# Block-diagonal scores for the last query tile, copies of keys on GpSimd, and 20 instead of 50 unread products

## The chip, the cores and the metric

The kernel runs on one core of one Trainium2 chip. The metric is the device time of one launch in microseconds. The engines are named as in the profile: PE (TensorE, products), PEld (its weight loads), DVE (VectorE), ACT (ScalarE), POOL (GpSimd) and SP (SyncE, which issues the DMAs).

## What is computed

Four batches of eight heads attend over 576 positions with a head size of 64 and a decay term, then two dense layers follow. Cut to what matters:

```
scores = scale * q @ k^T;  cum = cumsum(log(clip(f)))
scores = where(causal, -1e9, scores + cum[:, None] - cum[None, :])
attn = softmax(scores);  x = (attn @ v), heads side by side: 2304 x 512
h = x @ w_in;   g = h * clip(h + 3, 0, 6) / 6;   x = g @ w_out        # first layer, 512 -> 2048 -> 512
h = x @ w_in2;  g = piecewise square of h;       out = g @ w_out2     # second layer
```

## The kernel before, in words

**Attention.** The 576 queries of a head are cut at 256. The lower half of a batch gives four jobs of kind "two" (two heads, query tiles 0 and 1), the upper half gives for each pair of heads two jobs of kind "one" (one head, tiles 2 and 3) and one of kind "last". The fifth tile has 64 queries of each head only, so "last" handles both heads of a pair in one 128-row tile. There are 16 jobs of kind "two", 32 "one" and 16 "last". The 16 "two" jobs run their scores as fp32 products (`sc<-kn,qn`).

**Split operands.** In the upper halves an fp32 number is a rounded fp32r part (qh, the high part) and a rest (ql). A tile kk holds the 64 rows of the rounded keys above the 64 rows of their rest, and q stands twice above itself in qh and ql, so qh times kk gives qh·k_high + qh·k_rest in one product of 128 rows. A "last" tile needs qh and ql for two heads: q of each head was padded with zero columns to 128 columns (behind the 256 of qraw, hence the width QW), and four products for each half of the 288 keys add up to the scores: eight products 128x288 for a pair of heads.

**Dense layers.** `moe_h` makes a 128-wide piece of the hidden layer out of 12 products into a bank hp, ACT and DVE turn it into two parts g, and `moe_o` adds them into the output banks o. Weights come as raw 64-bit data and are split by ACT and DVE (`w_split`, wr and w).

**Order.** The program is written out as a list of pieces, and then `plan` records all instructions, builds their dependences (`graph`), gives each a cost in ns and lets a list scheduler (`schedule`) set the order on each engine, which the engines keep. `cost` and `late` are those of the planner. "held" names tiles whose DMA the planner may not put ahead of the PE instruction that stands before it in the program. SPARE products that nobody reads (`spare<-upper,lf`) are set by the planner where it sees PE idle. They share the two banks of `ps_h` with hp: as long as one is still to come, only one bank is free for hp. The dense products start once pairs 0 to 4 of the attention are through (av, then xt); the dense work of the first layer is interleaved with the rest of the attention.

Of the kernel before, what the change touches and what calls it, by code (L numbers as in the profile page):

```python
# [8 lines left out]
F32 = mybir.dt.float32  # L9
F32R = mybir.dt.float32r  # L10
# [6 lines left out]
P = 128  # L17
# [16 lines left out]
NATS = 16  # L34
QW = S - QA + (S - 4 * 128)
DB = 3
NORMS = 12
FIRST = 8
EARLY = 6
SPARE = 50  # L40
AHEAD0 = 1
# [59 lines left out]
def graph(nc, homes, follows, held=()):  # L101
# [119 lines left out]
    for k, i in enumerate(ops):  # L221
# [154 lines left out]
def tile_kernel(  # L376
# [83 lines left out]
    def w_split(kind, c, half, s, raw):  # L460
        if kind == "parts":
# [5 lines left out]

        nc.scalar.activation(out=rf, in_=hw.bitcast(F32), func=AF.Abs)  # L468
        nc.vector.tensor_scalar(
            out=rf, in0=rf, scalar1=2.0 ** -15, scalar2=122880.0,  # L470
            op0=ALU.max, op1=ALU.min,
        )
        nc.vector.tensor_scalar(
            out=t, in0=t, scalar1=5, scalar2=2, op0=ALU.logical_shift_left, op1=ALU.logical_shift_right
        )
        nc.vector.scalar_tensor_tensor(
            out=t, in0=hw, scalar=-1073741824, in1=t, op0=ALU.bitwise_and, op1=ALU.bitwise_or
        )
        nc.vector.scalar_tensor_tensor(  # L479
            out=t, in0=lw, scalar=29, in1=t,  # L480
            op0=ALU.logical_shift_right, op1=ALU.bitwise_or,
        )
        hi, lo = wsb[half][s][:, 0], wsb[half][s][:, 1]
# [26 lines left out]
    nc.gpsimd.memset(pt4, 0.0)  # L510

    def v_load(p):
        d = pairs[p]
# [7 lines left out]
    def u_load(n):  # L521
# [4 lines left out]
        if kind == "last":  # L526

            d["dec"] = att.tile([P, S], F32, tag="dec", name="dec", bufs=DB)
            for y in range(2):
                nc.sync.dma_start(out=d["dec"][y * D:(y + 1) * D], in_=ncum[r + y:r + y + 1, :].to_broadcast([D, S]))  # L530
            return
        q0, nq, nk = (0, QA, QA) if kind == "two" else (QA, S - QA, S)
# [9 lines left out]
        else:  # L542
            kraw = att.tile([P, S], F32, tag="kraw", name="kraw", bufs=1)
            qraw = att.tile([P, QW], F32, tag="qraw", name="qraw", bufs=1)
            for y in range(2):
# [3 lines left out]
                )  # L549
            if kind == "one":  # L550

                o = QA + W4 * (h % 2)
                nc.gpsimd.memset(qraw[:, S - o:S - o + W4], 0.0)
                nc.sync.dma_start(out=qraw[:, 0:QA], in_=q[b, h, :, q0:q0 + QA])
                nc.sync.dma_start(out=qraw[:, o:o + W4], in_=q[b, h, :, q0 + QA:S])
            d.update(kraw=kraw, qraw=qraw)
        w = nk if kind == "two" else 4 * P
        dec = att.tile([P, S], F32, tag="dec", name="dec", bufs=DB)
        if n < DECS:
            t = bank("dc")  # L560
            for y in range(nh):
                ty = t[:, y * QA:(y + 1) * QA]
                for c in range(QA // P):
# [3 lines left out]
                    )  # L567
            rounded("v", dec[:, 0:nh * nk], t[:, 0:nh * nk])
        else:
# [5 lines left out]
    def u_split(n):  # L575
# [3 lines left out]
        if kind == "last":  # L579
# [8 lines left out]
            )  # L588
            rounded("p", end[D:P], dm[D:P, 0:W4])
        else:  # L590

# [7 lines left out]
            if not d["nat"]:  # L599
# [4 lines left out]
                ql = att.tile([P, QW], F32R, tag="ql", name="ql", bufs=3)  # L604
                w, x = nh * d["nk"], 2 * QA if kind == "two" else QA + P
                rounded("a", kk[:, 0:w], kraw[:, 0:w])
                rest("v", kk[D:P, 0:w], kraw[D:P, 0:w], kk[D:P, 0:w])
                rounded("a", qh[:, 0:x], qraw[:, 0:x])
                rest("v", ql[:, 0:x], qraw[:, 0:x], qh[:, 0:x])
                d.update(kk=kk, qh=qh, ql=ql)  # L610
# [18 lines left out]
    def u_scores(n, i):  # L629
# [5 lines left out]
        if kind == "last":  # L635
# [3 lines left out]
            ts = [bank("sc") for _ in halves]  # L639
            for part in ("qh", "ql"):  # L640
                for t, (a, e) in zip(ts, halves):
                    for y in range(2):
                        o = jobs[n - 2 + y]
                        nc.tensor.matmul(  # L644
                            t[:, 0:e - a], lhsT=o[part][:, QA:QA + P], rhs=o["kk"][:, a:e],
                            start=part == "qh" and y == 0, stop=part == "ql" and y == 1,
                        )
            softmax(d, 0, pr, [(t[:, 0:e - a], dec[:, a:e], a, e) for t, (a, e) in zip(ts, halves)])
# [33 lines left out]
    def u_norm(n):  # L682
# [17 lines left out]
    def u_trans(n, x):  # L700
# [12 lines left out]
        if kind == "two":  # L713
# [3 lines left out]
            for y in range(2):  # L717
                for z, i in enumerate(tl):
                    tr(y * w + z * P, prob[i], y * (i * P + P) + x * P)
            rounded("a", pt[:, x, :, x * P:QA], t[:, 0:2 * w].rearrange("p (h n) -> p h n", h=2))  # L720
# [282 lines left out]
    nc.sync.dma_start(out=lf0, in_=f0)  # L1003
    lf = att.tile([P, L], F32, tag="prob1", name="lf")


# [68 lines left out]
    for g in range(len(steps) + LAG):  # L1075
# [21 lines left out]
        else:  # L1097
# [46 lines left out]
```

## Time and profile before

| | |
|---|---|
| median of 3 runs | 1003.04 us (1000.57 to 1003.18) |
| the profiled execution | 1000.51 us, span of its instructions 998.8 us |
| PE busy | 989.3 us (99% of the span) |
| DVE busy | 577.3 us (58%) |
| ACT busy | 523.0 us (52%) |
| POOL busy | 75.6 us (8%) |
| DMA | 129 MB, 40.2% of the DMA engines' span in the main queue |

Busy times are those of the engine's instructions, without the sequencer's waits and issues. The busy time of PE is modelled at its ends, so hidden waits of some tenths of a microsecond can lie in it. An fp32 product leaves two records in the trace, an fp32r product one.

### The profile page before, as it was taken

Reading aid. Unit: us, or ns where it says so; the run is one execution under the profiler, and the core shown is the slowest. Engines: PE = TensorE matmul, PEld = TensorE weight load, DVE = VectorE, ACT = ScalarE, POOL = GpSimd, SP = SyncE. Lnnn points to the kernel's source line nnn. Section 1 sums busy time; section 2 is a strip of 40 time slices with the busy share of each in tenths; the row PEclk is TensorE's granted clock in tenths of the full one; section 3 lists DMA queues with packets and bytes.
Section 4 is the critical chain, followed back from the end, with each engine's and each line's share of the span. In section 5 each row is a group of like instructions: output and inputs, shape, how many; then the busy total and the mean of one; then the engine's idle time right before and its main releaser. Section 6 shows DMA issues by size and latency. Waiting matters only on the chain.

```text
span 998.8 us, 14754 instructions
## 1 busy us (share of the span) xinstructions
PE 989.3 (99%) x5110; PEld 799.2 (80%) x5110; DVE 577.3 (58%) x1375; ACT 523.0 (52%) x1192; POOL 75.6 (8%) x208
## 2 busy tenths in 40 slices
PE   8999999999999999999999999999999999999998
PEld 6766777777778777779988888888888888888897
DVE  7799677899763655555436489997222322322232
ACT  6988566667763656555523256674333333433343
POOL 2121100111110101100000002001000000000000
PEclk9999999999999999999999999999999999999999
DMA  6773669745565875238382337342000100100010
GB/s 195 218 205 115 178 208 295 249 138 151 175 218 208 247 221 155 84 104 271 111 325 78 103 106 240 130 164 77 11 1 27 43 1 1 42 6 1 1 43 22
DMA packets 67099, 129.05 MB, mean 129 GB/s; under 512 B 11728, under 2 KB 32464, under 8 KB 67024
## 3 DMA queue, kind: packets, MB, share of 16 engines
q1 hardware_dynamic: 67024, 128.11, 40.2%
q8 instruction: 40, 0.66, 0.3%
q14 instruction: 35, 0.29, 0.1%
HBM read 102.84 MB, written 25.24 MB: 128 GB/s over the span
## 4 chain that ended last, share of the span: by engine, by line
PE 96%; DVE 1%; DMA 1%; issue 1%; ACT 0%; POOL 0%; SPq 0%; DVEq 0%; ACTq 0%; POOLq 0%
PE hp L849 40%; PE o L899 20%; PE o L892 19%; PE pt L711 4%; PE av L753 4%; PE sc L669 3%; PE sc L659 2%; PE sc L644 2%; PE spare L1017 1%; PE dc L564 1%; DMA wraw<-in_w 0%; DVE prob L619 0%; DMA dec<-ncum 0%; DMA lf<-in_f 0%; DVE kk L431 0%
## 5 line engine op out<-in xcount | busy, mean ns | idle before, releaser
L849 PE MATMUL hp<-xt,w 128*128 128x512 f32 (+1 forms) x960 | 229.2, 377 | 0.7 <-DVE u L857 0.7
L892 PE MATMUL o<-g,w 128*128 128x512 f32 (+1 forms) x960 | 227.9, 376 | 0.1
L849 PE MATMUL hp<-x,w 128*128 128x512 f32 (+1 forms) x960 | 210.6, 368 | 0.0
L899 PE MATMUL o<-w,g 128*128 128x512 f32 x864 | 209.6, 389 | 0.0
L849 PEld LDWEIGHTS hp<-x,w 128*128 128x128 f32 x960 | 169.3, 188 | 31.2
L849 PEld LDWEIGHTS hp<-xt,w 128*128 128x128 f32 x960 | 163.7, 189 | 30.5 <-issue 2.8
L892 PEld LDWEIGHTS o<-g,w 128*128 128x128 f32 x960 | 164.5, 189 | 29.1 <-issue 1.7
L899 PEld LDWEIGHTS o<-w,g 128*128 128x128 f32 x864 | 161.1, 188 | 32.8
L861 DVE SCALAR_TENSOR_TENSOR u<-hp,u 128x512 f32<-128x512 f32 (+1 forms) x80 | 50.9, 637 | 166.6 <-ACT u L860 166.6
L431 DVE TENSOR_TENSOR g<-u,g 128x512 fp32r<-128x512 f32 (+1 forms) x160 | 102.2, 639 | 62.9 <-ACT g L423 36.7
L423 ACT ACTIVATE g<-u 128x512 fp32r<-128x512 f32 (+1 forms) x160 | 94.2, 589 | 77.3 <-DVE u L861 49.5
L859 ACT ACTIVATE u<-hp 128x512 f32<-128x512 f32 (+1 forms) x80 | 44.3, 554 | 155.8 <-PE hp L849 155.8
L625 ACT ACTIVATE prob<-prob,mx 128x128 f32<-128x128 f32 (+4 forms) x144 | 83.6, 582 | 53.2 <-DVE mx L619 52.5
L857 DVE SCALAR_TENSOR_TENSOR u<-u,hp 128x512 f32<-128x512 f32 (+1 forms) x80 | 50.5, 631 | 85.3 <-ACT u L856 85.0
L856 ACT ACTIVATE u<-hp 128x512 f32<-128x512 f32 (+1 forms) x80 | 44.1, 551 | 95.2 <-PE hp L849 94.8
L619 DVE CUSTOM_DVE_ANT_0 prob<-sc,dec 128x256 f32<-128x256 f32 (+2 forms) x112 | 55.2, 502 | 37.1 <-PE sc L669 28.9
L423 ACT ACTIVATE pt<-pt 128x512 f32<-128x512 f32 (+3 forms) x160 | 63.2, 433 | 24.4 <-PE pt L711 23.9
L711 PE MATMUL pt<-ident,prob 128*128 128x128 f32 (+1 forms) x400 | 64.3, 275 | 0.2
L711 PEld LDWEIGHTS pt<-ident,prob 128*128 128x128 f32 (+1 forms) x400 | 46.8, 139 | 16.5 <-issue 3.2
L423 ACT ACTIVATE w<-wr 128x512 fp32r<-128x512 f32 x64 | 40.3, 630 | 26.2 <-DVE wr L479 25.9
L753 PE MATMUL av<-pt,vv 128*64 128x320 f32 (+3 forms) x448 | 50.3, 364 | 0.0
L468 ACT ACTIVATE wr<-wraw 128x512 f32<-128x512 f32 x64 | 42.6, 668 | 12.2 <-DVE w L431 7.6
(73 smaller groups left out, 858.7 us busy)
## 6 DMA issues: line engine op xcount, KB each, us to landing
wraw<-in_w SPq DMA_DIRECT2D x64, 512.0 KB, 4.2
w<-wf SPq DMA_DIRECT2D x40, 512.0 KB, 5.0
wf<-w SPq DMA_DIRECT2D x28, 512.0 KB, 5.7
dec<-ncum SPq DMA_DIRECT2D x44, 256.0 KB, 3.7
kraw<-in_k SPq DMA_DIRECT2D x64, 144.0 KB, 3.5
x2d<-osb SPq DMA_DIRECT2D x22, 256.0 KB, 3.9
vv<-in_v SPq DMA_DIRECT2D x16, 320.0 KB, 3.5
dec<-ncum SPq DMA_DIRECT2D x32, 144.0 KB, 3.4
```

The costliest lines, as they stand in the source:

```text
L423: nc.scalar.activation(out=out, in_=in_, func=AF.Copy)
L431: e.tensor_tensor(out=out, in0=in_, in1=hi.bitcast(F32), op=ALU.subtract)
L619: nc.vector.tensor_tensor_reduce(out=py[:, a:e], in0=s, in1=dc, scale=-0.125, scalar=mx[:, 2 * z:2 * z + 1] if x else 3.0e38, op0=ALU.add, ...
L625: nc.scalar.activation(out=py, in_=py, func=AF.Exp, scale=-1.0, bias=mx[:, 2 * z + x:2 * z + x + 1], accum_out=sm[:, z:z + 1],)
L711: nc.tensor.transpose(t[:nk, o:o + P], p[:, c:c + nk], ident)
L753: nc.tensor.matmul(t[y * D:(y + 1) * D, o:nq], lhsT=vv[:, y, c], rhs=rhs, start=c == 0, stop=c == nkc - 1,)
L849: nc.tensor.matmul(hp, lhsT=ws[:, a, k], rhs=x[:, bb, 0:w], start=(k == 0 and a == 0 and bb == 0), stop=(k == KD - 1 and bb == 1),)
L857: nc.vector.scalar_tensor_tensor(out=u, in0=u, scalar=6.0, in1=hp, op0=ALU.min, op1=ALU.mult)
L859: nc.scalar.activation(out=u, in_=hp, func=AF.Relu, bias=0.5, scale=0.5)
L861: nc.vector.scalar_tensor_tensor(out=u, in0=hp, scalar=1.0, in1=u, op0=ALU.max, op1=ALU.min)
L892: nc.tensor.matmul(o, lhsT=ws[:, a, k], rhs=gg[:, bb], start=(n and k % m == 0 and a == 0 and bb == 0), stop=(last and bb == 1 and k % m = ...
L899: nc.tensor.matmul(acc[j][k], lhsT=gg[:, bb, k * P:(k + 1) * P], rhs=ws[:, a].rearrange("p k n -> p (k n)"), start=(n and a == 0 and bb == ...
```

## The change

Each "last" job gets its q straight into a tile q4 that holds two 128-column matrices: a block-diagonal one (head y's 64 rows of q in the rows and columns of y) and one with the blocks crossed. Both are rounded by ACT (qh), and DVE makes the rest of the diagonal one (ql). GpSimd copies the rounded keys of both heads into one tile kx, head by head, and later the rest of the first head's keys over the second head's rounded keys in that head's kk. For this the odd head keeps its rest in the upper rows. The scores then take three products for each half: qh·kx, ql·kx, crossed qh·kk. The padded columns of q, their memsets and DMAs go (32 DMAs and 32 memsets); 64 small DMAs of 64x64 come. The unread products fall from 50 to 20. In the planner the costs of fp32 scores and unread products change, and DMAs of kraw and qraw are now "held". DIAG, CONV, DECA and RAWS are zero, so the code behind them is not run.

```diff
-QW = S - QA + (S - 4 * 128)
+QW = QA
-SPARE = 50
+SPARE = 20
...
-                c = 1.7 * cols if "sc" == o[0][:2] else max(120, cols * 0.82)
-            cost[k], late[k] = 2 * c if o[0][:2] == "dc" else c, 172
+                c = max(160, 1.7 * cols)
+            cost[k], late[k] = c, 172
...
+            for x in range(2):
+                for y in range(2):
+                    z = (x + y) % 2
+                    nc.sync.dma_start(
+                        out=q4[y * D:(y + 1) * D, x, z * W4:(z + 1) * W4], in_=q[b, h + z, y * D:(y + 1) * D, 4 * P:S]
+                    )
...
+            rounded("a", qh, q4.rearrange("p x n -> p (x n)"))
+            rest("v", ql[:, 0:P], q4[:, 0], qh[:, 0:P])
+            kx = att.tile([P, S], F32R, tag="kx", name="kx", bufs=1)
+            for y in range(2):
+                rounded("p", kx[y * D:(y + 1) * D], jobs[n - 2 + y]["kk"][y * D:(y + 1) * D].bitcast(F32))
...
-            for part in ("qh", "ql"):
-                for t, (a, e) in zip(ts, halves):
-                    for y in range(2):
-                        o = jobs[n - 2 + y]
-                        nc.tensor.matmul(
-                            t[:, 0:e - a], lhsT=o[part][:, QA:QA + P], rhs=o["kk"][:, a:e],
+            ky = jobs[n - 1]["kk"]
+            rounded("p", ky[D:P], jobs[n - 2]["kk"][D:P].bitcast(F32))
+            for t, (a, e) in zip(ts, halves):
+                for x, (l, r) in enumerate(
+                    ((d["qh"][:, 0:P], d["kx"]), (d["ql"][:, 0:P], d["kx"]), (d["qh"][:, P:2 * P], ky))
+                ):
+                    nc.tensor.matmul(t[:, 0:e - a], lhsT=l, rhs=r[:, a:e], start=x == 0, stop=x == 2)
...
-    plan(tc, nc, homes, {"ext": "att", "ps_o": "ps_i"}, ("wraw", "wf"))
+    plan(tc, nc, homes, {"ext": "att", "ps_o": "ps_i"}, ("wraw", "wf", "kraw", "qraw"))
```

The planner sets a new order on every engine. Three places show it; line numbers of the changed kernel differ from those before (L701 was L669, the scores of "one"; L937 was L892, the output products; L894 was L849, the hidden products).

On PE, before, around the scores of a "last" job (L644); L669 is the last product that reads the second head's kk, L849 fills the time.

```order
L669 MATMUL sc<-kk,qh 128x512
L669 MATMUL sc<-kk,ql 128x512
L849 MATMUL hp<-xt,w_6_119 128x512 x2
L644 MATMUL sc<-kk,qh 128x288 x2
L644 MATMUL sc<-kk,ql 128x288 x2
L849 MATMUL hp<-xt,w_6_119 128x512 x2
L644 MATMUL sc<-kk,qh 128x288 x2
L644 MATMUL sc<-kk,ql 128x288 x2
```

The same place on PE with the change, in a later pair of heads (`sc<-kk,qh` of L679 is the third product, which reads what GpSimd wrote last).

```order
L701 MATMUL sc<-kk,ql 128x512
L937 MATMUL o_4294<-g,w_8_130 128x512
L679 MATMUL sc<-kx,qh 128x288
L679 MATMUL sc<-kx,ql 128x288
L937 MATMUL o_4294<-g,w_8_130 128x512
L937 MATMUL o_4295<-g,w_8_130 128x512
L679 MATMUL sc<-kx,qh 128x288
L679 MATMUL sc<-kk,qh 128x288
L679 MATMUL sc<-kx,ql 128x288
L679 MATMUL sc<-kk,qh 128x288
```

Eight products became six, and between the L701 row and the first third product stand two products of kx and some dense ones.

On POOL with the change, around the first "last" job; `dm<-dec` and `dec<-dec` are the causal masks of a job, `kx<-kk` and `kk<-kk` the new copies.

```order
L607 AFFINE_SELECT dm<-dec 128x64
L611 AFFINE_SELECT dec<-dec 128x64
L429 TENSOR_SCALAR dec<-dm 64x64
L628 AFFINE_SELECT dm<-dec 128x128
L628 AFFINE_SELECT dec<-dec 128x128
L429 TENSOR_SCALAR kk<-kk 64x576
L429 TENSOR_SCALAR kx<-kk 64x576
```

The copy `kk<-kk` stands behind the masks of the next job (L628), which wait for that job's decay data; before, no copies of keys stood here, only masks and memsets.

On PE near the start, before: the unread products ahead of the fifth av (L753), and the first dense products (L849).

```order
L1017 MATMUL spare<-upper,lf_134 128x128 x14
L753 MATMUL av<-pt,vv 64x256 x2
L753 MATMUL av<-pt,vv 64x128 x2
L711 MATMUL pt<-ident,prob_575 128x128
L711 MATMUL pt<-ident,prob_603 128x128
L711 MATMUL pt<-ident,prob_575 128x128
L711 MATMUL pt<-ident,prob_603 128x128 x3
L659 MATMUL sc<-kn,qn 128x256 x2
L659 MATMUL sc<-kn,qn 128x128 x2
L849 MATMUL hp<-xt,w_0_113 128x512 x3
L1017 MATMUL spare<-upper,lf_134 128x128
L753 MATMUL av<-pt,vv 64x256 x2
```

With the change, the unread products ahead of the fifth av (L798).

```order
L750 MATMUL pt<-ident,prob_504 128x128 x2
L691 MATMUL sc<-kn,qn 128x128
L1063 MATMUL spare<-upper,lf_136 128x128 x6
L798 MATMUL av<-pt,vv 64x256 x2
L798 MATMUL av<-pt,vv 64x128 x2
L750 MATMUL pt<-ident,prob_575 128x128
```

And with the change, the first dense products (L894).

```order
L894 MATMUL hp<-xt,w_0_113 128x512 x3
L798 MATMUL av<-pt,vv 64x256 x2
L798 MATMUL av<-pt,vv 64x128 x2
L1063 MATMUL spare<-upper,lf_136 128x128 x2
L894 MATMUL hp<-xt,w_1_114 128x512 x3
L894 MATMUL hp<-xt,w_0_113 128x512 x2
```

The block of 14 became one of 6. In all, 41 unread products stood ahead of the first dense one, now 18; behind it 9, now 2, and the second piece of the hidden layer (w_1) starts right behind those two.

## Rows read from the trace of the kernel before

**Rows 1.** The page: busy time by engine, chain that ended last by line.

```profile
PE 989.3 (99%) x5110; PEld 799.2 (80%) x5110; DVE 577.3 (58%) x1375; ACT 523.0 (52%) x1192; POOL 75.6 (8%) x208
...
PE hp L849 40%; PE o L899 20%; PE o L892 19%; PE pt L711 4%; PE av L753 4%; PE sc L669 3%; PE sc L659 2%; PE sc L644 2%; PE spare L1017 1%; PE dc L564 1%; DMA wraw<-in_w 0%; DVE prob L619 0%; DMA dec<-ncum 0%; DMA lf<-in_f 0%; DVE kk L431 0%
```

**Rows 2.** Waits of PE: us in total, times, longest.

```profile
PE dc L564 <- DVE lf L1013: 3.4, 1, 3.4
PE hp L849 <- DVE u L857: 0.7, 1, 0.7
```

**Rows 3.** Windows: length, busy by engine (PE, PEld, DVE, ACT, POOL), PEclk, DMA.

```profile
15.00:42.20 27.20, 26.66 (x198) 19.61 (x196) 21.55 (x83) 25.26 (x85) 5.18 (x12) 1.00 0.70 200
42.20:65.00 22.80, 21.70 (x117) 14.49 (x116) 21.33 (x69) 19.65 (x59) 3.31 (x6) 1.00 0.67 200
110.00:500.00 390.00, 389.58 (x2185) 311.54 (x2185) 254.99 (x675) 231.30 (x578) 40.03 (x139) 1.00 0.60 190
```

**Rows 4.** Timeline of PE at the first "last" job: start, us, instruction.

```profile
128.64 0.69 PE L644 MATMUL sc<-kk,qh 128*128 128x288 f32 x4
129.16 0.70 PE L644 MATMUL sc<-kk,ql 128*128 128x288 f32 x4
129.70 1.09 PE L849 MATMUL hp<-xt,w 128*128 128x512 f32 x4
```

**Rows 5.** Timeline near the start: unread products and what follows them.

```profile
14.51 3.07 PE L1017 MATMUL spare<-upper,lf 128*128 128x128 f32 x26
17.42 0.27 PE L711 MATMUL pt<-ident,prob 128*128 128x128 f32 x1
...
35.57 3.39 PE L1017 MATMUL spare<-upper,lf 128*128 128x128 f32 x28
38.89 0.87 PE L753 MATMUL av<-pt,vv 128*64 128x256 f32 x8
...
36.96 0.85 ACT L423 ACTIVATE pt<-pt 128x512 f32<-128x512 f32 x2
```

**Rows 6.** Windows of the unread products alone: busy PE, busy PEld.

```profile
10.00:42.20 32.20, 11.28 (x82) 9.82 (x82) 1.00 0.74 219
42.20:65.00 22.80, 3.39 (x18) 2.62 (x18) 1.00 0.67 200
```

**Rows 7.** GpSimd's copies, line L425: duration ns min/median/max, forms.

```profile
L425 POOL TENSOR_SCALAR dec<-dm x16: 243/243/595, 117.1 to 480.0; 64x64 f32<-64x64 f32 x16
L425 POOL TENSOR_SCALAR x<-x x16: 405/624/1213, 616.0 to 854.9; 128x512 fp32r<-128x512 f32 x12, 128x256 fp32r<-128x256 f32 x4
```

**Rows 8.** Timeline: how PE hands on to DVE, and POOL to DVE.

```profile
126.10 0.40 PE L669 MATMUL sc<-kk,qh 128*128 128x512 f32 x1
...
126.33 0.39 PE L669 MATMUL sc<-kk,ql 128*128 128x512 f32 x1
126.87 0.69 DVE L619 CUSTOM_DVE_ANT_0 prob<-sc,dec 128x512 f32<-128x512 f32 x1 [0.72 <-PE sc L669]
...
564.45 0.62 POOL L425 TENSOR_SCALAR x<-part 128x512 fp32r<-128x512 f32 x1 [5.70 <-DVE part L836]
565.10 0.69 DVE L431 TENSOR_TENSOR x<-part,x 128x512 fp32r<-128x512 f32 x1 [0.80 <-POOL x L425]
```

**Rows 9.** Timeline: masks of the next job, and a "last" job's first product.

```profile
247.66 0.29 POOL L595 TENSOR_SCALAR_AFFINE_SELECT dec<-dec 128x128 f32<-128x128 f32 x1
249.78 0.43 PE L644 MATMUL sc<-kk,qh 128*128 128x288 f32 x2
```

**Rows 10.** DMA issues of padded q: count, KB each, us to landing.

```profile
qraw<-in_q SPq DMA_DIRECT2D x32, 32.0 KB, 3.2
```

**Rows 11.** Timeline of PE at the start, fp32 products 128x256 and 128x128.

```profile
3.37 4.37 PE L564 MATMUL dc<-upper,lf 128*128 128x256 f32 x16 [3.37 <-DVE lf L1013]
8.73 1.57 PE L564 MATMUL dc<-upper,lf 128*128 128x256 f32 x8
```

**Rows 12.** A window of low PE activity behind the start.

```profile
60.00:65.00 5.00, 3.96 (x16) 2.20 (x14) 5.00 (x14) 3.87 (x10) 1.62 (x2) 1.00 0.80 254
```

More of the change, by code (lines that the diff above doesn't have):

```diff
@@ L34 @@
 NATS = 16
-QW = S - QA + (S - 4 * 128)
+QW = QA
 DB = 3
 NORMS = 12
+DIAG = 0
+CONV = 0
+DECA = 0
+RAWS = 0
 FIRST = 8
 EARLY = 6
-SPARE = 50
+SPARE = 20
 AHEAD0 = 1
@@ L466, in w_split @@
         lw, hw = raw[:, :, 0], raw[:, :, 1]
[L468 to L482, printed above, removed]
+        if CONV == 1:
+            nc.vector.tensor_scalar(
+                out=rf, in0=hw.bitcast(F32), scalar1=2.0 ** -112, scalar2=1.0, op0=ALU.mult, op1=ALU.mult
+            )
+        elif CONV == 2:
+            nc.scalar.activation(out=rf, in_=hw.bitcast(F32), func=AF.Copy, scale=2.0 ** -112)
+        if CONV == 0:
+            nc.scalar.activation(out=rf, in_=hw.bitcast(F32), func=AF.Abs)
+            nc.vector.tensor_scalar(
+                out=rf, in0=rf, scalar1=2.0 ** -15, scalar2=122880.0,
+                op0=ALU.max, op1=ALU.min,
+            )
+            nc.vector.tensor_scalar(
+                out=t, in0=t, scalar1=5, scalar2=2, op0=ALU.logical_shift_left, op1=ALU.logical_shift_right
+            )
+            nc.vector.scalar_tensor_tensor(
+                out=t, in0=hw, scalar=-1073741824, in1=t, op0=ALU.bitwise_and, op1=ALU.bitwise_or
+            )
+            nc.vector.scalar_tensor_tensor(
+                out=t, in0=lw, scalar=29, in1=t,
+                op0=ALU.logical_shift_right, op1=ALU.bitwise_or,
+            )
+        else:
+            nc.vector.tensor_scalar(
+                out=t, in0=t, scalar1=3, scalar2=0, op0=ALU.logical_shift_left, op1=ALU.logical_shift_left
+            )
+            nc.vector.scalar_tensor_tensor(
+                out=t, in0=hw, scalar=-2147483648, in1=t, op0=ALU.bitwise_and, op1=ALU.bitwise_or
+            )
+            nc.vector.scalar_tensor_tensor(
+                out=t, in0=lw, scalar=29, in1=t, op0=ALU.logical_shift_right, op1=ALU.bitwise_or,
+            )
         hi, lo = wsb[half][s][:, 0], wsb[half][s][:, 1]
@@ L510, in tile_kernel @@
     nc.gpsimd.memset(pt4, 0.0)
+    q4 = att.tile([P, 2, P], F32, tag="q4", name="q4", bufs=1)
+    nc.gpsimd.memset(q4, 0.0)
     def v_load(p):
@@ L530, in u_load @@
                 nc.sync.dma_start(out=d["dec"][y * D:(y + 1) * D], in_=ncum[r + y:r + y + 1, :].to_broadcast([D, S]))
+            for x in range(2):
[3 more added lines that the diff above has]
+                        out=q4[y * D:(y + 1) * D, x, z * W4:(z + 1) * W4], in_=q[b, h + z, y * D:(y + 1) * D, 4 * P:S]
+                    )
             return
@@ L549, in u_load @@
                 )
[L550 to L555, printed above, removed]
+            nc.sync.dma_start(out=qraw, in_=q[b, h, :, q0:q0 + QA])
             d.update(kraw=kraw, qraw=qraw)
@@ L567, in u_load @@
                     )
-            rounded("v", dec[:, 0:nh * nk], t[:, 0:nh * nk])
+            rounded("a" if n < DECA else "v", dec[:, 0:nh * nk], t[:, 0:nh * nk])
         else:
@@ L589, in u_split @@
             rounded("p", end[D:P], dm[D:P, 0:W4])
+            qh = att.tile([P, QW], F32R, tag="qh", name="qh", bufs=3)
+            ql = att.tile([P, QW], F32R, tag="ql", name="ql", bufs=3)
+            rounded("a", qh, q4.rearrange("p x n -> p (x n)"))
[3 more added lines that the diff above has]
+                rounded("p", kx[y * D:(y + 1) * D], jobs[n - 2 + y]["kk"][y * D:(y + 1) * D].bitcast(F32))
+            d.update(qh=qh, ql=ql, kx=kx)
         else:
@@ L604, in u_split @@
                 ql = att.tile([P, QW], F32R, tag="ql", name="ql", bufs=3)
[L605 to L609, printed above, removed]
+                o = 0 if d["hs"][0] % 2 else D
+                rounded("a", kk, kraw)
+                rest("v", kk[o:o + D], kraw[o:o + D], kk[o:o + D])
+                rounded("a", qh, qraw)
+                rest("v", ql, qraw, qh)
                 d.update(kk=kk, qh=qh, ql=ql)
@@ L639, in u_scores @@
             ts = [bank("sc") for _ in halves]
-            for part in ("qh", "ql"):
-                for t, (a, e) in zip(ts, halves):
-                    for y in range(2):
-                        o = jobs[n - 2 + y]
-                        nc.tensor.matmul(
-                            t[:, 0:e - a], lhsT=o[part][:, QA:QA + P], rhs=o["kk"][:, a:e],
-                            start=part == "qh" and y == 0, stop=part == "ql" and y == 1,
-                        )
+            ky = jobs[n - 1]["kk"]
[5 more added lines that the diff above has]
+                    nc.tensor.matmul(t[:, 0:e - a], lhsT=l, rhs=r[:, a:e], start=x == 0, stop=x == 2)
             softmax(d, 0, pr, [(t[:, 0:e - a], dec[:, a:e], a, e) for t, (a, e) in zip(ts, halves)])
@@ L689, in u_norm @@
         nc.vector.reciprocal(out=rd[:, 0:k], in_=sm[:, 0:k])
+        if n < DIAG:
+            d["diag"] = att.tile([P, S], F32, tag="prob2", name="diag")[:, 0:4 * P].rearrange("p (z n) -> p z n", z=4)
+            nc.gpsimd.affine_select(
+                out=d["diag"], in_=rd.unsqueeze(2).to_broadcast([P, 4, P]), compare_op=ALU.is_equal, fill=0.0, base=0,
+                pattern=[[0, 4], [-1, P]], channel_multiplier=1,
+            )
+            return
         for j, i in enumerate(d["tiles"]):
@@ L718, in u_trans @@
                 for z, i in enumerate(tl):
-                    tr(y * w + z * P, prob[i], y * (i * P + P) + x * P)
+                    o, c = y * w + z * P, y * (i * P + P) + x * P
+                    if "diag" in d:
+                        nc.tensor.matmul(
+                            t[:, o:o + P], lhsT=prob[i][:, c:c + P], rhs=d["diag"][:, 2 * y + i], start=True, stop=True,
+                        )
+                    else:
+                        tr(o, prob[i], c)
             rounded("a", pt[:, x, :, x * P:QA], t[:, 0:2 * w].rearrange("p (h n) -> p h n", h=2))
@@ L1004, in tile_kernel @@
     lf = att.tile([P, L], F32, tag="prob1", name="lf")
+    weights_ahead(-1, RAWS)
     upper = att.tile([P, QA], F32, tag="upper", name="upper", bufs=1)
```

## The prediction

> **What bounds the kernel now.** I read the page first: PE is busy for 989.3 us, 99% of the span, and the chain that ended last runs through PE products almost throughout [rows 1]. Busy PE could still hide waits, so I read the waits of PE next: one of 3.4 us before the first product, then nothing above 0.7 us [rows 2]. The windows tell where other engines matter. From 110 to 500 us, where all the "last" jobs lie, PE is busy for 389.58 of 390 us while DVE and ACT have over a third of their time free [rows 3]: there time is the sum of PE's products, and a product less is its length less. Before 65 us it is otherwise: ACT is busy for 25.26 of 27.2 us up to 42.2 us, and DVE for 21.33 of 22.8 us from there to 65 us, and much of what PE does there is unread products [rows 3, 6]. There the attention's softmax and the splitting of weights set the pace, and a shorter PE list need not end earlier.
>
> **Term 1, the scores.** Two of eight products go in each of 16 "last" jobs, 32 in all. Eight of them took from 128.64 to 129.70 us, 0.1325 us each, with the next dense product right behind [rows 4]. 32 x 0.1325 = 4.2 us, and since PE has no gap there, I take all of it: -4.2.
>
> **Term 2, the unread products.** An unread product is two records; 13 of them took from 14.51 to 17.42 us, 0.224 us each [rows 5]. 30 fewer are 6.7 us of PE at most. Of the 30, 23 stood before the first dense product and 7 behind it. What they hid: the block of 14 ends at 38.89 us with the fifth av, whose last input ACT had ready at 36.96 + 0.85 = 37.81 us, so that block was about 1.1 us too long; the block of 13 ends when its successor's input came [rows 5]. Taking unread products away there brings the rest forward only as far as ACT has idle time, 27.2 - 25.26 = 1.9 us to 42.2 us, and DVE behind that, 22.8 - 21.33 = 1.5 us to 65 us [rows 3]. What goes beyond those 3.4 us would have to come from dense products that PE makes in the freed time: the second hidden bank is free earlier, but its pieces need weights that DVE splits, and DVE is full. I take -2.0, a bit over half of 3.4; the ends are 0 (PE waits where it computed for nobody) and -6.7. Wherever less than the whole comes back, the page after shows PE idle in the place of the unread products.
>
> **Term 3, the wait for GpSimd.** The third product of a "last" job waits for a copy 64x576 that may start only when the last product of the job before has read kk. No such copy is in the trace; the nearest are 128x512 at 0.62 us undisturbed and 64x64 at 0.243 us [rows 7, 8]. From them the slope is (0.62 - 0.243)/448 = 0.84 ns per column, so 64x576 takes an estimated 0.67 us undisturbed. DVE took up a result of PE 0.54 us after the start of a product 128x512 (126.33 to 126.87), and one of POOL 0.03 us after its end [rows 8]. So the third product can start 0.54 + 0.67 + 0.03 = 1.24 us after the start of that last reader. What PE has to do meanwhile is counted from the new order with 0.1325 for a 288, 0.23 for a 512 product (from 126.10 to 126.33 us, [rows 8]) and half of that for a 256: 12 of the 16 jobs have 1.31 to 1.40 us, four have 1.85 us or more. Undisturbed, nobody waits. But copies of GpSimd took up to 1.213 us instead of 0.62 [rows 7]; with 1.213 + 0.05 for 64 more columns the third product could start 1.83 us after, 0.5 us late in the 12 jobs, 6 us in all; where the copy begins late behind a disturbed one a bit more. The median of the 16 wide copies is 0.624 us, so most are undisturbed; I take 0.1 us for each of 12 jobs: +1.2, with ends at 0 and +6.
>
> The copy also stands on POOL behind the masks of the next job, which wait for a DMA. In the narrowest place that I found, the second mask had ended at 247.95 us and the "last" products began at 249.78 us [rows 9], so I take nothing for it; if that DMA came 2 us later, PE would wait with it, and with PE everything.
>
> [...]
>
> **Work costed at nothing.** ACT rounds 256 instead of 384 columns of q for each "one" job and 256 more for each "last"; DVE's rests likewise: about even, and under PE from 110 us on. The first two copies of each "last" (kx) come a job earlier, and POOL is busy for only 40.03 of 390 us [rows 3]; 48 x 0.67 = 32 us more fit, and if they didn't, the kx copies would join term 3. Against 32 padded DMAs [rows 10] come 64 small ones on SP, 32 more in all; they are loaded two jobs ahead, and without that lead each would put its landing of some 3.2 us in front of a "last". Their places and the held loads of kraw and qraw also move weights' loads forward at the start, which I leave inside term 2. The rest of the new order I count at 0, plus or minus 1.
>
> **Sum.** -4.2 - 2.0 + 1.2 = -5.0. On the profiled execution that is 1000.51 - 5.0 = 995.5. That execution lay 2.5 us below the median of the runs, so for the median I forecast 1003.04 - 5.0 = 998.0.
>
> **Rivals.**
> *The unread products come back whole* (0.13). For it: all PE time behind 65 us is dense work, so anything PE does earlier counts. Against it: DVE and ACT are full. -4.2 - 6.7 + 1.2: 993.3.
> *Nothing comes back at the start, and the copies cost more* (0.20). PE waits where it made unread products, and each of the 12 jobs waits 0.25 us: -4.2 + 3.0: 1001.8, within the measurement.
> *PE waits for GpSimd in earnest* (0.09). The slower side. With nothing from the start, the waits must eat 4.2 us and 3.0 more: 7.2/12 = 0.6 us a job, just above the 0.5 of the longest copy, and easily reached if a mask ahead of the copy waits for its DMA. At 0.7 us: 1003.0 - 4.2 + 8.4 = 1007.2. Against it: the masks are early [rows 9] and most copies undisturbed [rows 7].
> *PE slows at the start* (0.07). [...]
> [...]
>
> **Chances and range.** The forecast has 0.51, the rivals 0.13, 0.20, 0.09 and 0.07. About 0.3% (3.0 us) is what a measurement of this kernel can tell from no change. Faster takes the forecast's case nearly whole and the first rival, 0.63; same the second and half of the fourth and a little of the forecast's upper end, 0.26; slower the third and a part of the fourth, 0.11. The likeliest case alone reaches from 995 to 1001. The range has to take in most of the whole return at the start and the second rival: 992.0 to 1003.5; what is left out are the two slower rivals and the lowest edge.
>
> **What would show it.** Right: six products 128x288 in each "last" at 0.133 us; 40 records of unread products; the first dense product at 40 to 42 us instead of 42.2; PE idle a little before 65 us and hardly any wait of `sc` on POOL behind 110 us, a tenth each. Wrong: a line "PE sc <- POOL kk" of more than 3 us in the waits; PE's early products at twice their length behind 10 us; DVE above 0.9 busy behind 110 us. It would also be wrong if the new order of the DMAs let dense products wait for weights.

## The result and the profile after

The changed kernel takes 1010.38 us (median of 6 runs, 1007.39 to 1010.83) against 1002.39 us of the kernel before (6 runs beside it and alone): a ratio of 1.0077, interval 1.0063 to 1.0091. It is slower, where 998.0 us was forecast. The profiled execution is the fastest, 1007.39 us at a mean granted clock of 1.000; the other five had 0.996 to 0.998.

The page: busy time by engine, and the lines of the chain that ended last.

```profile
PE 988.1 (98%) x5018; PEld 786.8 (78%) x5018; DVE 588.3 (58%) x1391; ACT 523.7 (52%) x1208; POOL 123.8 (12%) x225
...
PE 61%; DVE 9%; issue 2%; DMA 2%; ACT 2%; POOL 0%; DVEq 0%; SPq 0%; POOLq 0%; ACTq 0%
```

PE has 92 records less than in [rows 1] (32 scores with one record each and 30 unread products with two) and is still as good as always busy, yet the span is 6.8 us longer, and DVE is busy for 11 us more, though it has only 16 instructions more. PE's share of the chain that ended last is 61%; in the kernel before it is 96%. The windows, with the stretches and columns of [rows 3]:

```profile
15.00:42.20 27.20, 25.02 (x172) 16.72 (x170) 24.04 (x95) 26.97 (x93) 5.91 (x12) 1.00 0.73 215
42.20:65.00 22.80, 20.07 (x97) 12.69 (x97) 20.78 (x63) 18.81 (x54) 3.28 (x6) 1.00 0.67 199
110.00:500.00 390.00, 386.05 (x2109) 301.35 (x2110) 261.04 (x673) 226.29 (x574) 87.56 (x155) 1.00 0.61 191
```

The start went nearly as forecast: PE pauses where it made unread products, and the first dense product starts at 39.67 us instead of 42.23 (40 to 42 had been named). The loss lies in the long stretch, where PE had no gap: 3.95 us not busy instead of 0.42, and 76 records fewer done in the same time, of which only 32 are the scores that no longer exist. The waits of PE (us in total, times, longest; compare [rows 2]):

```profile
PE sc L701 <- DVE kk L435: 2.0, 7, 0.3
PE hp L894 <- DVE u L902: 1.9, 1, 1.9
PE sc L691 <- DVE mx L652: 1.2, 3, 0.6
PE sc L701 <- DVE ql L435: 1.0, 5, 0.3
```

The scores of the "one" jobs (L701) wait for the rests of keys and queries, kk and ql, of which the kernel before shows no wait at all. The view of the tile kk (duration ns min/median/max, first and last start):

```profile
L429 POOL TENSOR_SCALAR kx<-kk x32: 664/988/1597, 108.1 to 496.0; 64x576 fp32r<-64x576 f32 x32
...
L435 DVE TENSOR_TENSOR kk<-kraw,kk x32: 733/755/1224, 108.6 to 496.0; 64x576 fp32r<-64x576 f32 x32
...
L429 POOL TENSOR_SCALAR kk<-kk x16: 672/675/891, 125.6 to 503.4; 64x576 fp32r<-64x576 f32 x16
```

In the kernel before no rest from 110 to 500 us took longer than 760 ns:

```profile
L431 DVE TENSOR_TENSOR kk<-kraw,kk x30: 755/756/760, 114.2 to 472.6; 64x576 fp32r<-64x576 f32 x30
```

With the change a rest kk takes up to 1224 ns, the kx copy has a median of 988 ns where its shortest is 664, and the ky copy (kk<-kk), on which the prediction spent its care, has a median of 675 ns and is mostly undisturbed. One collision in the timeline (start, us, instruction, idle before):

```profile
141.58 0.67 ACT L427 ACTIVATE kk<-kraw 128x576 fp32r<-128x576 f32 x1
...
142.33 1.15 POOL L429 TENSOR_SCALAR kx<-kk 64x576 fp32r<-64x576 f32 x1 [4.54 <-ACT kk L427]
...
142.85 1.22 DVE L435 TENSOR_TENSOR kk<-kraw,kk 64x576 fp32r<-64x576 f32 x1
...
144.22 0.41 PE L701 MATMUL sc<-kk,qh 128*128 128x384 f32 x1 [0.26 <-DVE kk L435]
```

ACT's rounding of kk releases two readers: GpSimd's copy and DVE's rest. The copy starts first, the rest takes 1.22 instead of 0.755 us, and PE's product starts 0.15 us behind it. Here two things come together: the rest is made just in time, and the copy is in its way. From the 32 "one" jobs' starts and ends: a rest of keys ended a median of 9.0 us before its first product in the kernel before, and 0.16 us in the changed one; 17 of the 32 products start 0.14 to 0.16 us behind the rest, as the one above does, where 3 did before. The loads of kraw are "held", so they, ACT's rounding and DVE's rest all come later in the order.

### The profile page after: what moved, and what is told of

Read it like the earlier page. It is cut to its first block, busy times and chain, and to the rows that moved or that the text cites. A ratio compares the mean times of both kernels' runs of the same rounds, so it can differ in the third digit from the quotient of the medians.

```text
span 1005.6 us, 14665 instructions
## 1 busy us (share of the span) xinstructions
PE 988.1 (98%) x5018; PEld 786.8 (78%) x5018; DVE 588.3 (58%) x1391; ACT 523.7 (52%) x1208; POOL 123.8 (12%) x225
## 4 chain that ended last, share of the span: by engine, by line
PE 61%; DVE 9%; issue 2%; DMA 2%; ACT 2%; POOL 0%; DVEq 0%; SPq 0%; POOLq 0%; ACTq 0%
PE hp L894 26%; PE o L944 17%; PE o L937 10%; PE av L798 3%; PE pt L750 2%; PE sc L701 2%; DVE wr L487 1%; DVE wr L490 1%; DMA wraw<-in_w 1%; DVE w L435 1%; DVE g L435 1%; PE sc L679 1%; DVE wr L480 1%; DVE prob L652 1%; DVE wr L484 1%
## 5 line engine op out<-in xcount | busy, mean ns | idle before, releaser
L894 PE MATMUL hp<-xt,w 128*128 128x512 f32 (+1 forms) x960 | 233.4, 376 | 2.0 <-DVE u L902 1.9
L937 PE MATMUL o<-g,w 128*128 128x512 f32 (+1 forms) x960 | 229.3, 375 | 0.0
L894 PE MATMUL hp<-x,w 128*128 128x512 f32 (+1 forms) x960 | 211.3, 368 | 0.4 <-DVE w L435 0.3
L894 PEld LDWEIGHTS hp<-x,w 128*128 128x128 f32 x960 | 169.0, 188 | 32.5 <-DVE w L435 1.4
L894 PEld LDWEIGHTS hp<-xt,w 128*128 128x128 f32 x960 | 164.7, 189 | 31.5 <-issue 2.7
L937 PEld LDWEIGHTS o<-g,w 128*128 128x128 f32 x960 | 164.9, 189 | 29.2 <-issue 1.7
L652 DVE CUSTOM_DVE_ANT_0 prob<-sc,dec 128x256 f32<-128x256 f32 (+2 forms) x112 | 55.5, 500 | 53.5 <-PE sc L701 41.5
L429 POOL TENSOR_SCALAR kx<-kk 64x576 fp32r<-64x576 f32 x32 | 32.1, 1004 | 168.3 <-ACT kk L427 168.3
L798 PE MATMUL av<-pt,vv 128*64 128x320 f32 (+3 forms) x448 | 50.4, 364 | 0.4 <-ACT pt L427 0.3
```

The source lines that it names most:

```text
L652: nc.vector.tensor_tensor_reduce(out=py[:, a:e], in0=s, in1=dc, scale=-0.125, scalar=mx[:, 2 * z:2 * z + 1] if x else 3.0e38, op0=ALU.add, ...
L798: nc.tensor.matmul(t[y * D:(y + 1) * D, o:nq], lhsT=vv[:, y, c], rhs=rhs, start=c == 0, stop=c == nkc - 1,)
L894: nc.tensor.matmul(hp, lhsT=ws[:, a, k], rhs=x[:, bb, 0:w], start=(k == 0 and a == 0 and bb == 0), stop=(k == KD - 1 and bb == 1),)
L937: nc.tensor.matmul(o, lhsT=ws[:, a, k], rhs=gg[:, bb], start=(n and k % m == 0 and a == 0 and bb == 0), stop=(last and bb == 1 and k % m = ...
```

## The experiments

The theories at this point: **late loads** (the held list cost the rests their lead), **copies** (GpSimd's copies lengthen DVE's work), and as rivals the **third product** of the "last" jobs, PE's new order, or the missing unread products.

**The held list and the copies, one at a time.** Three edits of the changed kernel: the held list as before (e1), the kx copies cut to 64 columns (e3), and both (e5). In e3 and e5 the other columns of kx are zero, so the scores of the last tile leave most keys out, and the planner is still given the cost of the long copies.

```diff
 e1, e5
-    plan(tc, nc, homes, {"ext": "att", "ps_o": "ps_i"}, ("wraw", "wf", "kraw", "qraw"))
+    plan(tc, nc, homes, {"ext": "att", "ps_o": "ps_i"}, ("wraw", "wf"))
 e3, e5
-  rounded("p", kx[y * D:(y + 1) * D], jobs[n - 2 + y]["kk"][y * D:(y + 1) * D].bitcast(F32))
+  rounded("p", kx[y * D:(y + 1) * D, 0:W4], jobs[n - 2 + y]["kk"][y * D:(y + 1) * D, 0:W4].bitcast(F32))
```

e1: 

> The changed kernel with the loads of kraw and qraw no longer held (the planner's list is again wraw and wf). Theory L (late loads): in the trace of the changed kernel the rest of the keys ends 0.15 us ahead of the first product that reads it in most of the 32 jobs of kind one, before the change a median 9 us ahead; holding the loads took that lead away. Then the lead is back here, the waits of the scores of kind one for DVE's rests fall from 3.0 us to under 0.5 us, and the time falls by 6 to 9 us, to 1001 to 1004. Theory C (contention): the copies of GpSimd slow DVE's rests, whenever they come; then the waits stay near 3 us and the time stays within 2 us of 1010. Theory G (the third product waits for GpSimd, as in the prediction's third rival): no change.

e3: 

> The changed kernel, but the two kx copies of each last job are 64x64 instead of 64x576; the other columns of kx stay zero, so the scores of the last tile are left wrong. The planner is given the cost of the long copies, so the order on PE, DVE, ACT and SP is that of the changed kernel, and only GpSimd's busy time falls, by about 32 x 0.75 = 24 us. Theory C: the rests of the keys are no longer slowed (0.755 instead of 0.915 us on average), the waits for them go, and the time falls by 5 to 8 us. Theory L: the rests still come just in time by the plan, only less late; the time falls by 1 to 3 us. Theory G: the copy on which the third product waits is unchanged, and so is the time.

e5: 

> The changed kernel with the loads of kraw and qraw not held and with GpSimd copies of 64 columns in place of 576 (the last tile's scores then read mostly zeros: part of the last tile's work is left out of GpSimd, none of TensorE's); orders on the other engines as in the run with loads not held (1000.98 us). Theories A and B (late loads and copies explain the loss): the 4.2 us of the saved products and some of the 1.7 us of the start come back, 994.5 to 997.5 us, and pt waits for prob no longer than before (under 1 us in all). Theory C: 1000 to 1002 us as with whole copies.

And three of the kernel before: the held list of the change alone (e2), 32 copies into a tile that nobody reads (e8), both (e8b).

```diff
 e2, e8b
-    plan(tc, nc, homes, {"ext": "att", "ps_o": "ps_i"}, ("wraw", "wf"))
+    plan(tc, nc, homes, {"ext": "att", "ps_o": "ps_i"}, ("wraw", "wf", "kraw", "qraw"))
 e8, e8b: behind the masks of "last"
+  kx = att.tile([P, S], F32R, tag="kx", name="kx", bufs=1)
+  for y in range(2):
+      rounded("p", kx[y * D:(y + 1) * D], jobs[n - 2 + y]["kk"][y * D:(y + 1) * D].bitcast(F32))
```

e2: 

> The kernel before with one edit: its loads of kraw and qraw are held as in the changed kernel. There are no copies of keys on GpSimd, eight products for a last job and 50 unread products. Theory L: the rests come just in time here too, the scores of kind one wait for DVE, and the time rises by 3 to 7 us, to 1005 to 1010. Theories C and G: nothing on GpSimd changed, so the time stays within 2 us of 1002.4.

e8: 

> The kernel before with only the two GpSimd copies of rounded keys (64x576 each, 32 in all) added ahead of each pair's last tile, into a tile that no product reads; the order on TensorE, VectorE, ScalarE and the DMA queue stays that of the kernel before, keys' rests stay some 9 us ahead of their products. Theory A (copies cost only where rests come just in time): 1000.5 to 1002.5 us, no new waits for DVE kk. Theory B (the copies slow VectorE and that costs by itself, as the waits for prob in the run with the loads not held suggest): 1004 to 1007 us with waits of pt for prob. Theory C (not the copies at all, but the new order of products): as the kernel before, 1001 us, and the same in the next run as in the one of held loads.

e8b: 

> The kernel before with the held kraw and qraw loads and the 32 unread GpSimd copies, everything else as before; order on the other engines is that of the run with only the held loads (1004.55 us, ratio 1.003). Theory A: the two together cost more than their sum, 1008 to 1012 us, with waits of the one-head scores for DVE kk as in the changed kernel. Theory B: their sum, 1007 to 1010 us. Theory C: 1004 to 1005 us, nothing added by the copies.

Measured, with the median, the ratio to the kernel before and its interval. The last two columns are worked out from the starts of PE's products between 65 and 525 us: by how much the pauses from start to start ahead of a product exceed the median that e5 has for the same pair, added up for the products "pt" and for the "one" scores.

```
                          us       ratio  interval          pauses ahead of pt, one (us)
four products (before)
  held list (e2)          1004.55  1.0030 1.0017..1.0043    6.0   5.2
  copies (e8)             1006.18  1.0057 1.0045..1.0069    7.2   3.3
  both (e8b)              1010.81  1.0095 1.0082..1.0108    7.3   9.5
  neither (before)           -     1         -              3.5   3.0
three products (change)
  neither (e5)             995.61  0.9946 0.9934..0.9958    3.6   2.4
  held list (e3)          1003.23  1.0016 1.0003..1.0029    7.8   4.6
  copies (e1)             1000.98  0.9996 0.9984..1.0009    8.9   2.7
  both (after)            1010.38  1.0077 1.0063..1.0091    7.5  10.3
```

Without late loads and wide copies the rest of the change (three products, fewer unread ones, the new order) brings 0.54%, 5.4 us. The copies take back 0.50% (e5 to e1) or, without the change, 0.57% (e8). The held list takes 0.30% alone (e2) and 0.70% with three products (e5 to e3). Both together cost about their sum: the four results of the lower half add up to -5.4 + 5.0 + 7.0 = +6.6 us against +7.7 measured, those of the upper half to 3.0 + 5.7 = 8.7 against 9.5. So neither is harmless without the other; the first theory that I formed for e8, that copies cost only where rests are just in time, fell. In the traces PE, DVE and ACT run the same instructions in the same order in e5 and e1, in e3 and the changed kernel, in the kernel before and e8, and in e2 and e8b, so each of these pairs differs by GpSimd's work alone. The rivals aren't needed for the loss: e8b has eight products, no third one and 50 unread products, and e8 has PE's old order besides.

What differs is who waits. In e8 the lead of the rests is still 9.4 us. Its waits of PE, and its tile kk:

```profile
PE pt L714 <- DVE prob L701: 1.5, 6, 0.3
...
PE sc L672 <- DVE kk L431: 0.4, 1, 0.4
```

```profile
L425 POOL TENSOR_SCALAR kx<-kk x32: 663/672/1240, 101.3 to 480.9; 64x576 fp32r<-64x576 f32 x32
...
L431 DVE TENSOR_TENSOR kk<-kraw,kk x32: 755/755/1244, 102.9 to 480.0; 64x576 fp32r<-64x576 f32 x32
```

Here the copies also hit the normalisation of the softmax, and its transposes (pt) wait. Its view in the kernel before, then in e8, from 110 to 500 us:

```profile
L698 DVE TENSOR_SCALAR prob<-prob,rd x84: 279/479/571, 112.8 to 496.9; 128x384 f32<-128x384 f32 x32, 128x512 f32<-128x512 f32 x32, 128x576 f32<-128x576 f32 x16, 128x128 f32<-128x128 f32 x2
...
L701 DVE TENSOR_SCALAR prob<-prob,rd x85: 280/478/931, 109.9 to 489.0; 128x384 f32<-128x384 f32 x31, 128x512 f32<-128x512 f32 x31, 128x576 f32<-128x576 f32 x15, 128x128 f32<-128x128 f32 x4
```

The timeline of one:

```profile
158.46 1.02 POOL L425 TENSOR_SCALAR kx<-kk 64x576 fp32r<-64x576 f32 x1 [8.92 <-DVE kk L431]
158.87 0.93 DVE L701 TENSOR_SCALAR prob<-prob,rd 128x576 f32<-128x576 f32 x1
...
159.95 0.63 PE L714 MATMUL pt<-ident,prob 128*128 128x128 f32 x4 [0.23 <-DVE prob L701]
```

In e1 it is the same, and this wait is by far the longest left in its list behind 110 us:

```profile
PE pt L750 <- DVE prob L737: 2.9, 9, 0.7
```

In e5 neither wait is there, and PE is busy throughout the stretch of [rows 3]:

```profile
110.00:500.00 390.00, 389.99 (x2201) 312.88 (x2202) 252.49 (x693) 233.22 (x596) 66.27 (x154) 1.00 0.61 190
```

In e2 and e3, with the loads late, the rests' lead is 0.16 and 0.27 us, and from 110 to 520 us the listed waits of PE come to 0.4 and 0.5 us in all; the loss is many small pauses, which only the last two columns of the table show. Only part of them is where the first theory looked: against its partner without the held list, e2 has 2.2 us more ahead of "one" and 2.5 ahead of pt, e3 2.2 and 4.2. The products pt don't read the rests, and why they come later under the held list is not shown. Two signs of the theory of late loads failed with it: e2's list hardly has the waits for DVE, and e3 takes 6 to 7 us less than the changed kernel, where late loads alone would have given 1 to 3.

**The unread products.** e7 is the kernel before with 20, e4 the changed one with 45 (with 50 the planner finds no order for it).

```diff
 e7                          e4
-SPARE = 50                 -SPARE = 20
+SPARE = 20                 +SPARE = 45
```

e7: 

> The kernel before with 20 unread products in place of 50 and nothing else; 27 lines of TensorE's order differ, which are those products. If the unread products had stood in the way of real work at the start: 996.5 to 999 us (-2 to -4 us, and the lead is kept to the end). If the start is bound by the weights' arrival and conversion and the unread products only filled gaps: 1000 to 1002 us, a ratio within 0.999 to 1.002. Slower by over 2 us only if TensorE's granted clock falls in the first 60 us.

Measured: 1002.36 us, ratio 1.0009 (0.9997 to 1.0020): nothing gained. The first dense product starts at 42.4 us, as before, and in the windows of e7 the granted clock (third figure from the right) is what [rows 3, 12] never showed:

```profile
15.00:42.20 27.20, 23.71 (x160) 16.39 (x160) 21.58 (x83) 25.50 (x87) 5.18 (x12) 0.94 0.69 203
42.20:55.00 12.80, 12.61 (x61) 7.13 (x58) 12.16 (x42) 11.04 (x35) 1.24 (x2) 0.86 0.62 186
60.00:65.00 5.00, 4.02 (x12) 2.06 (x11) 4.97 (x13) 3.87 (x10) 0.38 (x1) 0.78 0.73 227
65.00:70.00 5.00, 5.00 (x23) 3.50 (x23) 3.42 (x12) 3.73 (x12) 0.80 (x2) 0.88 0.40 142
```

All 12 runs of e7 had a mean clock of 0.992 to 0.998, while 14 of the 17 runs of the kernel before beside it had 0.999 or 1.000 (median 1000.86 us; the other three took 1003.16, 1003.38 and 1005.82 us). So with 30 unread products fewer the granted clock was below 1 for part of the start, 0.78 to 0.94 in four of the windows above. Among e7's own runs the time goes from 1005.06 us at a mean clock of 0.992 to 1000.24 at 0.998, so that is what eats what their absence gives. Here the unread products do a job.

e4: 

> The changed kernel with 45 unread products instead of 20 (50 can't be placed by its planner). Theory L, C and G: only the start moves; the time rises by 0 to 4 us. If the lower number of unread products had cost PE its rate at the start, the time would fall by 2 us or more.

Measured: 1024.56 us, ratio 1.0236 (1.0219 to 1.0253). It tells little: the planner makes a wholly other order of it. At 511 us it is 4.5 us behind the changed kernel, and from there to 690 us it loses 12.5 us more; the longest waits of PE there, 4.5 us in all, are of dense products for weights that ACT rounds late.

**What of a copy is in DVE's way.** The unread copies of e8 replaced by memsets, which write as much and read nothing (e13), and by copies of 8 columns with such a memset behind each (e14).

```diff
 e13, in place of e8's copies
+      nc.gpsimd.memset(kx[y * D:(y + 1) * D].bitcast(F32), 0.0)
 e14, in place of e8's copies
+      rounded("p", kx[y * D:(y + 1) * D, 0:8], jobs[n - 2 + y]["kk"][y * D:(y + 1) * D, 0:8].bitcast(F32))
+      nc.gpsimd.memset(kx[y * D:(y + 1) * D].bitcast(F32), 0.0)
```

e13: 

> The kernel before with 32 GpSimd memsets of 64x576 at the places where the earlier run had its 32 unread copies of keys; the order on the other four engines is that of the kernel before. If what costs 5 us in the copies is that GpSimd reads SBUF (or reads and writes) while VectorE works on SBUF alone: 1000 to 1002.5 us, and VectorE's prob<-prob,rd and kk rests at their times of before. If any long GpSimd work there costs the same (by its writes, or by its place in GpSimd's queue ahead of the masks): 1004 to 1007 us.

Measured: 1016.74 us, ratio 1.0150 (1.0133 to 1.0168), and no answer to the question. The memsets depend on nothing, so all 32 started in the first 24 us, ahead of what else GpSimd had to do there; the first av came at 36.6 us instead of 20.9.

e14: 

> The kernel before with the 32 unread copies cut to 8 columns, each followed by a memset of 64x576 of the same tile, so that GpSimd starts at the same places of the program and is busy for about as long (572 ns for the memset against 664 ns for an undisturbed copy), but almost only writes. If the copies cost by what they read while VectorE reads two operands from SBUF: kk<-kraw,kk stays near 756 ns beside a memset and the time is 1000.5 to 1003 us. If by GpSimd's time at that place, or by its writes as much as by its reads: 1004 to 1007 us, with VectorE's instructions lengthened as in the run with copies.

Measured: 1002.55 us, ratio 1.0016 (1.0004 to 1.0028). The view of its tile kx, and of DVE's rests kk and normalisations prob from 110 to 500 us:

```profile
L425 POOL TENSOR_SCALAR kx<-kk x32: 191/202/764, 99.6 to 475.6; 64x8 fp32r<-64x8 f32 x32
L593 POOL MEMSET kx<- x32: 572/575/831, 99.9 to 476.2; 64x576 f32 x32
```

```profile
L431 DVE TENSOR_TENSOR kk<-kraw,kk x30: 755/756/766, 115.2 to 474.7; 64x576 fp32r<-64x576 f32 x30
```

```profile
L702 DVE TENSOR_SCALAR prob<-prob,rd x84: 282/480/884, 113.8 to 499.1; 128x384 f32<-128x384 f32 x32, 128x512 f32<-128x512 f32 x32, 128x576 f32<-128x576 f32 x16, 128x128 f32<-128x128 f32 x2
```

With memsets the rests keep their 756 ns (766 at most, against up to 1244 in e8), the normalisations go up to 884 ns, and the loss falls from 0.57% to 0.16%. So most of what the copies cost here goes with their reading.

**Versions that move GpSimd's copies.** In all of them the loads of kraw and qraw are not held, as before. e6: the kx copies on ACT; e9: by DMA; e10: by DMA, and ky on ACT; e11: all three by DMA; e12: e10 with 32 unread products.

```diff
 e6: rounded("a", kx..., ...) in place of rounded("p", ...)
 e9, e10, e11, e12
+  nc.sync.dma_start(out=kx[y * D:(y + 1) * D].bitcast(F32), in_=jobs[n - 2 + y]["kk"][y * D:(y + 1) * D].bitcast(F32))
 e10, e12: rounded("a", ky[D:P], ...) in place of rounded("p", ...)
 e11
+  nc.sync.dma_start(out=ky[D:P].bitcast(F32), in_=jobs[n - 2]["kk"][D:P].bitcast(F32))
```

e6: 

> The changed kernel with the loads of kraw and qraw not held and the two early key copies of a pair on ScalarE in place of GpSimd; the planner moves 204 lines of TensorE's order. Theory B (GpSimd's copies hold up VectorE's instructions that read only SBUF): the held-up instructions go back to their old times, 995 to 998 us, less what 32 ScalarE copies of some 0.5 to 0.7 us cost there (ScalarE is busy 59% of 110 to 500 us). Theory that any engine's 32 copies cost the same (one more step ahead of the last tile): 1000 to 1002 us, as with GpSimd's.

e9: 

> The changed kernel with the loads not held and the two early key copies of a pair made by DMA from SBUF to SBUF in place of GpSimd; the third copy (ky) stays on GpSimd. Theory B: VectorE's instructions keep their undisturbed times except beside the 16 ky copies, 994.5 to 998 us. If instead one more step ahead of the last tile is what costs, or the queue of loads is pushed back by 32 transfers of 147 KB: 1000 to 1004 us.

e10: 

> As the last one, with the third copy (ky, which the third product waits for) on ScalarE in place of GpSimd, so that GpSimd copies nothing. Theory B: what the 16 ky copies held up is gained too, up to 2 us under the last one (993 to 997 us), unless ScalarE is late with ky: then waits of sc for ACT kk and up to 2 us over it.

e11: 

> All three copies by DMA, loads not held. Theory B: as the two before while the planner can place the ky transfer early enough, 993 to 998 us; a transfer takes over 2 us from issue to landing where the GpSimd copy takes 0.7, so the third products may wait: waits of sc for DMA kk, up to 16 x 1 us, 1000 us or more.

e12: 

> The fastest whole version so far (loads not held, two key copies by DMA, the third on ScalarE: 997.86 us) with 32 unread products in place of 20; the planner moves 254 lines of TensorE's order. If the granted clock of 0.68 in 60 to 65 us there comes from too few unread products and costs what is missing to the run with short copies (995.6 us): 995.5 to 997.2 us at a clock of 1.0 in that stretch. If the unread products don't decide it: 997.5 to 999.5 us, the clock below 1.0 there as before.

```
      us       ratio   interval
e6     999.45  0.9981  0.9971..0.9992
e9     998.44  0.9969  0.9959..0.9978
e10    997.86  0.9967  0.9955..0.9980
e11   1001.28  0.9999  0.9990..1.0008
e12    998.81  0.9967  0.9955..0.9980
```

e6 gains only 0.15% on e1 (0.9996), less than expected; what its copies cost on ACT and what its new order does isn't parted. e10 beats both kernels, by 3.3 us and some 11 us. Its rests keep their time:

```profile
L435 DVE TENSOR_TENSOR kk<-kraw,kk x30: 731/753/757, 114.5 to 467.9; 64x576 fp32r<-64x576 f32 x30
```

It misses e5 by 2.2 us. e12 tells that this isn't the clock at the start: with 32 unread products the clock of 60 to 65 us is 1.00 instead of 0.68, and the ratio the same. The pauses ahead of pt and "one" in e10 are 4.2 and 3.6 us, 1.8 us more together than in e5; whether the new order or the DMAs make them stays open, as does why e11 loses 3.4 us more.

## Why the prediction was wrong

**The step that failed is "Work costed at nothing".** It put the kx copies at 0 because POOL was idle; that is the wrong engine to look at. They cost 0.50 to 0.57% (e1 against e5, e8), 5 to 6 us, most of it by what they do to DVE. And it left the held loads of kraw and qraw "inside term 2", as something at the start, with "the rest of the new order" at 0, plus or minus 1: they cost 0.30 to 0.70% (e2, e3 against e5), in small pauses all along the attention. Neither was among the rivals, whose slower one had the waits at the third product.

For the copies, the prediction weighed a disturbance for the ky copies alone, which are mostly undisturbed (median 675 ns), and took its size from 16 copies of another stage [rows 7]. The traces tell what the kx copies disturb: in e8, the 11 rests kk that overlap a copy take a mean of 882 ns against 755 for the other 21, the 128x384 normalisations 728 (6) against 419 (26), while prob<-sc,dec of 128x512, which reads PSUM, has 692 against 688. In e14 the rests, which read two tiles in SBUF, take at most 766 ns, the normalisations up to 884 where the kernel before has at most 571. Why the one is spared and the other isn't is not shown.

**Term 1 fits**: the six products 128x288 of the first "last" stand 0.13 us apart as in [rows 4], and e5 gains 5.4 us (4.2 to 6.6 by its interval) where term 1 has 4.2; what of e5's gain comes from the start and the new order, no run parts. **Term 2 was wrong in its cause.** Alone, 30 unread products fewer bring nothing (e7), the lower end of its range; the 2.6 us at the start came with the held list and the new order (the first dense product starts at 41.5 us with the held list and 50 unread products, e2, and at 40.5 with the new order and 20 but without the held list, e1). The rival *PE slows at the start* was nearer than its 0.07: it is what cancels the term in e7 (ratio 1.0009), and five of the six runs of the changed kernel have a mean clock of 0.996 to 0.998 and take 2.5 to 3.4 us more than the one at 1.000. Where the clock fell in those five no trace shows. Nor does a run show how slow PE gets in that rival, on which its place in the chances depends; in e7 the granted clock was 0.78 to 0.94 in four windows of the start. **Term 3 was right in size by luck**: pauses ahead of the "last" products are 2.8 us from 65 to 525 us by the measure of the table, 1.7 before; +1.1 against +1.2. But its cause was another: e1 and e5, with the same third copy, have 1.6, so these pauses too come with the late loads. The list of PE's waits has none for GpSimd; only five of its weight loads (PEld) waited for ky:

```profile
PEld sc L679 <- POOL kk L429: 2.0, 5, 0.5
```

The third product that stands right behind the longest ky copy, of 891 ns, starts at 214.29 us, 0.08 us late.

So the changed kernel is 5.4 us better by all but the wide copies and the held list, some 5 to 6 worse by the copies and 7 to 8 by the held list; the clock is a part of the loss in five of its six runs.

## What to carry to other kernels

In a kernel whose bound engine has no gap, delaying loads can cost as much as a saving of work brings, here 3 to 7 us against 5.4, and mostly in pauses too short for a list of waits: before delaying a load, measure from the trace how far ahead of its reader what is made of it is finished. Work on an idle GpSimd wasn't free here: its copies, which read SBUF, took VectorE's rests of two SBUF operands from 755 ns to as much as 1244 (e8), and the time up by 0.57%. Before placing such work, look for what else the same producer releases at that moment. Change a planner's rules one at a time: here a gain of 5.4 us lay under two losses, and the larger one, the held list, had nothing to do with it.

## What was unexpected of the hardware

An 8-column copy on GpSimd, 191 ns alone, took up to 764 ns in e14; one of 0.76 us began 0.05 us behind a rest of DVE and ended 0.05 us behind it, so that it took as long as the rest. How long each took went with who came first. In the changed kernel 28 kx copies overlap a rest kk. In 13 of these pairs the rest started first, by 0.01 to 0.13 us: it took 0.74 to 0.76 us, and the copy 1.16 to 1.60, where the shortest took 0.664. In the other 15 the copy started first, by 0.09 to 0.63 us, and the rest took up to 1.22 us and ended 0.59 to 0.66 us behind the copy. Twice the same pair in e8, apart by 0.05 and 0.03 us:

```profile
117.28 0.76 DVE L431 TENSOR_TENSOR kk<-kraw,kk 64x576 fp32r<-64x576 f32 x1
117.33 1.23 POOL L425 TENSOR_SCALAR kx<-kk 64x576 fp32r<-64x576 f32 x1 [3.53 <-ACT kk L423]
...
232.21 0.67 POOL L425 TENSOR_SCALAR kx<-kk 64x576 fp32r<-64x576 f32 x1 [4.36 <-ACT kk L423]
232.24 1.24 DVE L431 TENSOR_TENSOR kk<-kraw,kk 64x576 fp32r<-64x576 f32 x1
```

The clock fell around a short pause of PE, but not around every one. In e9 PE was busy for 3.78 of the 5 us from 60 to 65 us, and the granted clock of that stretch was 0.66; from 65 to 70 us it was 1.00 again. With 32 unread products (e12) PE paused from 55 to 60 us instead, 4.17 of 5 us busy, and the clock stayed at 1.00. In the profiled execution of the changed kernel it stayed there too, though PE paused for 1.92 us and was busy for only 3.03 of the 5 us from 55 to 60 us. What decides it is not shown. First e9, then the changed kernel:

```profile
60.00:65.00 5.00, 3.78 (x11) 3.05 (x12) 5.00 (x11) 2.46 (x4) 1.13 (x2) 0.66 0.77 244
...
55.00:60.00 5.00, 3.03 (x11) 1.67 (x11) 4.83 (x10) 3.47 (x8) 1.31 (x2) 1.00 0.62 178
60.00:65.00 5.00, 5.00 (x22) 3.52 (x21) 4.83 (x14) 3.76 (x10) 0.00 (x0) 1.00 0.62 226
```
